# Mixture-of-experts stage: weight pieces released by the count of matrix products instead of in queue order with tiny transfers between

## The chip, the cores and the metric

One core of one Trainium2 chip runs the whole kernel. The metric is the device time of one execution in microseconds (us), as the median of several runs. One execution was also recorded by the hardware profiler; that is the profiled execution of the tables below.

## The reference, cut to what matters

The program is windowed attention followed by a mixture of experts. The change touches only the second half, the experts' two products:

```python
def _moe_ref(x, w_gate, w1, w2, capacity):            # x [3072, 512], 8 experts, F = 1024
    ...
    for e in range(E):
        ...                                           # at most capacity = 80 tokens an expert
        h = np.maximum(x[tok_idx] @ w1[e], 0.0)       # w1[e] [512, 1024]
        out[tok_idx] = gate_w[tok_idx, None] * (h @ w2[e])   # w2[e] [1024, 512]
```

The weights are float32: 8 experts x 2 matrices x 2 MB = 32 MB, read once from HBM.

## The kernel before, in words

The kernel has an attention stage (to about 190 us of the profiled execution), a short stage that ranks the tokens of each expert, and the expert stage, which the change is about.

**The experts' weights.** Each of the 16 matrices is loaded in two halves of 1 MB, each half in four pieces of 128 partitions x 512 float32 (256 KB): 32 halves, 128 pieces. The list `wsrc` (line 289) gives the order: w1 of expert 0, w1 of 1, w2 of 0, w1 of 2, w2 of 1 and so on. `load_weight` (line 298) takes the next half of that list, finds it a place, and issues its four transfers on SyncE's queue (line 320). There are 17 places for 32 halves (`NA, NB, NC = 6, 7, 4`, line 252): six in `wpool`, seven that come free in the attention's key and value buffers and beside them, four in `wpool3`, opened at the start of the expert stage (line 1295). Half n from 17 on takes the place of half n - 17, and its transfer waits until the products that read the old half are done. The first 13 halves are loaded during the attention and ranking stages; line 1196 issues one piece of a half and keeps the other three in the list `owed_parts`, which `load_owed` (line 330) issues later. 19 halves, 76 pieces, are left for the expert stage.

**The tiny transfers.** In the expert stage the list `spaced` is set (line 1306). Then `load_weight` issues, after some of the pieces, a transfer of a single float32 from `wg_t` in HBM to a small tile `spaced` (lines 321 to 325): three after every five pieces, so that of eight transfers in the queue five are weight pieces. Nothing reads that tile.

**The start of the expert stage.** GpSimd gathers the 80 token rows of an expert with an indirect DMA (`gather`, line 1309) into one of three buffers. Between the gathers of experts 1 and 2 and after them, `load_weight(hold=True)` puts a one-element memset on GpSimd's queue (line 313) that writes the place of the new half; the half's transfers must follow it, so they start after the gathers have been issued. Four halves are issued this way in the stage's head (lines 1315 to 1320); then SyncE loads a register with the flag for the fallback path (line 1321), and the rest of the halves are issued as `need` (line 1334) calls for them in program order.

**The products.** `ffn1(e)` (line 1361) computes h = relu(x w1) of one expert: 2 halves x 4 row blocks x 4 contraction blocks x 2 column halves = 64 calls of `pe.matmul` (line 1374). `ffn2(e)` (line 1381) computes the second product, again 64 calls (line 1392). The inputs are float32, and in the profile each call shows as two weight loads into the array (PEld) and two matmuls (PE). "Product" below means one call. There are 16 such stages of 64 products, in the order of `wsrc`: ffn1(0), ffn1(1), ffn2(0), ffn1(2), ffn2(1) and so on (lines 1434 to 1445). Stage j reads halves 2j and 2j + 1. Between them TensorE transposes gathered tokens (`tokens`, line 1347) and results (`rows`, line 1413). ScalarE applies the relu after each half of ffn1 (line 1378), and GpSimd writes finished rows with an indirect DMA (line 1426).

**What sets the order.** In the expert stage the order on every engine is the order of the program text (`manual_schedule`, lines 1303, 1307 and 1432); the scheduler adds the waits that the data need. SyncE's queue holds only the weight pieces and the tiny transfers there; gathers and writes are GpSimd's.

Of the kernel before, what the change touches and what calls it, by code (L numbers as in the profile page):

```python
# [8 lines left out]
F32 = mybir.dt.float32  # L9
# [10 lines left out]
B, H, S, D = 4, 8, 768, 64  # L20
# [3 lines left out]
P = 128  # L24
# [219 lines left out]
def attention_moe(ctx: ExitStack, tc, q, k, v, n_sink, window, w_gate, w1, w2, capacity, q_t, k_t, v_t, vs_t, wg_t, out):  # L244
    nc = tc.nc
# [50 lines left out]
    spaced = []  # L296

    def load_weight(hold=False, now=4):
# [13 lines left out]
        if hold:  # L312
            po.memset(t[0:1, 0:1], 0.0)
        to = t.rearrange("p (c f) -> p c f", c=src.shape[1])
        for n, i in enumerate(range(0, 2 * F, DM)):
            c, f = divmod(i, src.shape[2])
            if n >= now:
                owed_parts.append((to[:, c, f:f + DM], src[:, c, f:f + DM]))
                continue
            nc.sync.dma_start(to[:, c, f:f + DM], src[:, c, f:f + DM])  # L320
            if spaced:
                j = spaced[0]
                if 3 * (j + 1) // 5 > 3 * j // 5:
                    nc.sync.dma_start(spaced[1][0:1, j:j + 1], wg_t[0:1, 0, 0:1])
                spaced[0] += 1
# [968 lines left out]
    with ExitStack() as fctx:  # L1294
# [11 lines left out]
        spaced += [0, sm.tile([1, 4 * len(wsrc)], F32, name="spaced")]  # L1306
# [8 lines left out]
        for e in range(NG):  # L1315
            gather(e)
            if e > 0:
                load_weight(hold=True)
        while len(wtiles) < NA + NB + NC:
            load_weight()  # L1320
# [12 lines left out]

        def need(which, e):
            while (which, e, 1) not in wtiles:
                load_weight()
# [24 lines left out]
        def ffn1(e):  # L1361
# [3 lines left out]
            for half in range(2):  # L1365
# [5 lines left out]
                for f, c in todo:  # L1371
                    fc = half * (HC // 2) + f
                    for m in range(2):
                        pe.matmul(ph[m * D:(m + 1) * D, f], columns(0, e, c, fc * P + m * D), x[:, c],  # L1374
                                  start=(c == 0 and not (wide and f)), stop=(c == DC - 1), skip_group_check=True)
# [5 lines left out]
        def ffn2(e):  # L1381
# [6 lines left out]
            for dc in range(DC):  # L1388
                to = last if dc == DC - 1 else py
                for k in range(HC):  # L1390
                    for m in range(2):
                        pe.matmul(to[m * D:(m + 1) * D, dc], columns(1, e, k, dc * P + m * D), h[:, k],  # L1392
                                  start=(k == 0), stop=(k == HC - 1), skip_group_check=True)
                    if final and dc == DC - 1 and k == HC // 2:
                        rows_first(e)
# [38 lines left out]
        for e in range(E):  # L1434
            ffn1(e)
            if e % 2:
                for n in range(e + 1, min(e + 3, E)):
                    need(0, n)
# [65 lines left out]
```

## Time and profile before

| what | us |
|---|---|
| median of 3 runs | 292.58 (292.45 to 292.86) |
| the profiled execution's own time | 289.65 |
| span of its instructions | 287.9 |
| first product of the expert stage starts | 199.38 |
| last matmul starts | 281.88 |

All times of rows and of the text are counted from the start of the span of the profiled execution. PE is TensorE's matmul, PEld its load of weights into the array, DVE VectorE, ACT ScalarE, POOL GpSimd, SP SyncE; a q behind the name means the engine's queue of instructions (SPq). "L320" is line 320 of the kernel before. "x64" counts instructions. "<- issue" names idle time in which the engine waited for nothing that the profile shows. In the views of DMA, q1 holds the transfers of SyncE's queue, q0 the indirect ones of GpSimd, and q8 and q14 the engines' instructions; the last column is the time of their packets as a share of the 16 DMA engines' time.

### The profile page before, as it was taken

The numbers are of one execution on the slowest core, as the hardware profiler recorded it, in microseconds if no ns is written. First come the engines' busy times: TensorE is split into PE (matmuls) and PEld (weight loads), VectorE is DVE, ScalarE is ACT, GpSimd is POOL, SyncE is SP. The second block draws the span as 40 slices with busy tenths as digits, with TensorE's granted clock in tenths as the row PEclk, the third lists the DMA queues.
The fourth block names the chain that finished last, engine by engine and source line by source line (L and its number), as shares of the span: only waits on it lengthen the run. The fifth ranks groups of instructions, "written<-read, shape, count | busy, mean of one in ns | idle before, by whom it ended". The sixth has DMA issues, their size and how long they took to land.

```text
span 287.9 us, 11256 instructions
## 1 busy us (share of the span) xinstructions
PE 267.1 (93%) x4401; PEld 208.5 (72%) x4401; DVE 168.7 (59%) x566; ACT 165.9 (58%) x670; POOL 160.3 (56%) x365
## 2 busy tenths in 40 slices
PE   7889999999999999999899999998998999999991
PEld 2456777667776666776577767655988999999990
DVE  7678978778898988989996997880010010100001
ACT  3967988888988888785778787720111121221220
POOL 5876988668898679589758686636120030020211
PEclk9999999999999999999999999999999999999997
DMA  7999680999562999864275915597989899999811
GB/s 171 361 307 339 276 289 11 316 284 321 215 226 73 277 304 419 314 204 143 74 259 181 317 54 186 184 292 249 301 269 277 279 307 336 307 310 306 261 57 34
DMA packets 33366, 69.76 MB, mean 242 GB/s; under 512 B 4250, under 2 KB 6426, under 8 KB 32922
## 3 DMA queue, kind: packets, MB, share of 16 engines
q1 hardware_dynamic: 32282, 66.34, 69.4%
q0 software_dynamic: 1024, 2.62, 3.0%
q8 instruction: 37, 0.61, 0.9%
q14 instruction: 23, 0.19, 0.2%
HBM read 55.05 MB, written 13.89 MB: 239 GB/s over the span
## 4 chain that ended last, share of the span: by engine, by line
PE 36%; issue 21%; DVE 19%; ACT 14%; POOL 5%; DMA 3%; SPq 1%; ACTq 0%; POOLq 0%; DVEq 0%
ACT prob L607 9%; PE sc L570 7%; PE ph L1374 7%; PE pp L623 6%; PE xp L664 6%; DVE nm L597 3%; PE py L1392 3%; DVE sc L590 3%; ACT pt L635 3%; DVE gt L850 2%; POOL out_dram L1426 2%; DVE gt L847 2%; DMA kv_w<-in_moe_w_dram 1%; PE pr L697 1%; DVE sc L587 1%
## 5 line engine op out<-in xcount | busy, mean ns | idle before, releaser
L607 ACT ACTIVATE prob<-sc,nm 128x132 f32<-128x132 f32 (+1 forms) x192 | 68.9, 376 | 10.1 <-DVE nm L597 9.8
L570 PE MATMUL sc<-kv,q 64*64 64x196 f32 (+2 forms) x768 | 47.5, 335 | 8.0 <-ACT prob L607 6.0
L597 DVE TENSOR_REDUCE nm<-sc 128x2 f32<-128x264 f32 (+1 forms) x96 | 41.4, 431 | 3.3
L570 PEld LDWEIGHTS sc<-kv,q 64*64 64x64 f32 x768 | 21.3, 133 | 29.4 <-ACT prob L607 19.1
L635 ACT COPY pt<-pp 128x512 f32<-128x512 f32 x48 | 28.1, 585 | 24.1 <-PE pp L623 19.1
L590 DVE COPY_PREDICATED sc<-upper,sc 128x256 f32<-128x256 int8 x80 | 33.7, 422 | 13.0 <-PE sc L570 6.4
L607 ACT ACTIVATION_READ_ACCUMULATOR prob<-sc,nm 128x1 f32 x192 | 40.3, 210 | 0.0
L664 PE MATMUL xp<-pt,kv 128*64 128x128 f32 x384 | 37.0, 285 | 0.0
L643 POOL TENSOR_SCALAR_AFFINE_SELECT own<-pt 128x512 f32<-128x512 f32 (+1 forms) x48 | 27.6, 575 | 11.3 <-ACT pt L635 10.8
L1426 POOL DMA_INDIRECT out_dram<-y,idx x8 | 7.3, 918 | 44.8 <-ACT y L1420 40.4
L1357 DVE COPY xs<-px 128x320 f32<-128x320 f32 x7 | 3.2, 487 | 49.3 <-PE px L1352 49.3
L623 PE MATMUL pp<-ident,prob 128*128 128x128 f32 x192 | 31.4, 286 | 0.1
L664 PE MATMUL xp<-own,kv 128*64 128x128 f32 x320 | 31.1, 273 | 0.0
L650 POOL TENSOR_SCALAR_AFFINE_SELECT pt<-pt 128x512 f32<-128x512 f32 (+1 forms) x48 | 28.5, 593 | 3.3
L623 PEld LDWEIGHTS pp<-ident,prob 128*128 128x128 f32 x192 | 20.2, 141 | 13.6 <-issue 9.1
L1374 PE MATMUL ph<-xs,w 128*64 128x80 f32 x640 | 26.4, 233 | 0.6 <-issue 0.4
L1392 PE MATMUL py<-h,w 128*64 128x80 f32 x640 | 25.5, 233 | 0.8 <-issue 0.8
L714 POOL TENSOR_TENSOR xr<-xr,rs 128x512 f32<-128x512 f32 x21 | 22.4, 1067 | 5.9 <-ACT xr L702 5.8
L1378 ACT ACTIVATE h<-ph 128x320 f32<-128x320 f32 x16 | 7.0, 437 | 31.7 <-PE ph L1374 31.7
L1374 PEld LDWEIGHTS ph<-xs,w 128*64 128x64 f32 x640 | 24.1, 137 | 1.2 <-issue 0.8
L1392 PEld LDWEIGHTS py<-h,w 128*64 128x64 f32 x640 | 23.5, 137 | 1.7 <-issue 1.6
L1311 POOL DMA_INDIRECT xg<-x_rows,idx_in x8 | 7.9, 994 | 28.3 <-PE px L1352 26.2
(194 smaller groups left out, 532.2 us busy)
## 6 DMA issues: line engine op xcount, KB each, us to landing
w<-in_moe_w_dram SPq DMA_DIRECT2D x80, 256.0 KB, 4.7
kv_w<-in_moe_w_dram SPq DMA_DIRECT2D x48, 256.0 KB, 4.6
kv<-in_v_t_dram SPq DMA_DIRECT2D x12, 512.0 KB, 8.8
out_dram<-zeros SPq DMA_DIRECT2D x24, 256.0 KB, 5.4
x_rows<-xr SPq DMA_DIRECT2D x24, 256.0 KB, 2.1
q<-in_q_t_dram SPq DMA_DIRECT2D x11, 512.0 KB, 9.9
kv<-in_k_t_dram SPq DMA_DIRECT2D x3, 1584.0 KB
kv<-in_k_t_dram SPq DMA_DIRECT2D x2, 528.0 KB
```

The costliest lines, as they stand in the source:

```text
L570: pe.matmul(sc[m * D:(m + 1) * D, h, c0:c1], qs[g][r, hp, q0:q0 + D], ks[b][r, hp, k0 + c0:k0 + c1], start=True, stop=True, skip_group_che ...
L590: ve.copy_predicated(own, upper, sc[:, :, 0:P])
L597: ve.tensor_reduce(out=nm, in_=sc[:, :, lo_c:hi_c], axis=AX.X, op=ALU.max, negate=True)
L607: ac.activation(prob[:, a, h, p0:], sc[:, h, lo_c:hi_c], AF.Exp, bias=nm[:, h:h + 1], scale=1.0, accum_out=ssum[:, n, 2 * hp + h:2 * hp + ...
L623: pe.transpose(pp[:, a, h], prob[:, a, h, SINK:], ident)
L635: ac.copy(pt, st.pop((t, "pp")))
L643: po.affine_select(out=own[:, a0:], in_=pt[:, a0:], pattern=[[0, 2 - a0], [0, 2], [1, P]], compare_op=ALU.is_ge, fill=0.0, base=0, channel ...
L650: po.affine_select(out=pt[:, a0:], in_=pt[:, a0:], pattern=[[0, 2 - a0], [0, 2], [-1, P]], compare_op=ALU.is_gt, fill=0.0, base=0, channel ...
L664: pe.matmul(xp[h * D:(h + 1) * D, a * P:(a + 1) * P], val[:, (2 * hp + h) * D:(2 * hp + h + 1) * D], pr[:, a, h], start=False, stop=(a == ...
L714: po.tensor_tensor(xr, xr, gst[(i0, "rs")][:, n, :, None].to_broadcast([P, H, D]), ALU.mult)
L1374: pe.matmul(ph[m * D:(m + 1) * D, f], columns(0, e, c, fc * P + m * D), x[:, c], start=(c == 0 and not (wide and f)), stop=(c == DC - 1), ...
L1392: pe.matmul(to[m * D:(m + 1) * D, dc], columns(1, e, k, dc * P + m * D), h[:, k], start=(k == 0), stop=(k == HC - 1), skip_group_check=True)
```

## The change

The tiny transfers, the memsets that held the first halves back, and the issue of four halves at the head of the stage go. Every product of the expert stage now goes through `product`, which counts it. After each eleventh, `next_piece` hands out the next piece: it takes the first of `owed_parts` (opening the next half with `load_weight(now=0)` if that list is empty and the place of the half is free by the count of products), issues its transfer on SyncE's queue, and gives the scheduler a dependency of that transfer on the product. `need`, which is still called ahead of each stage, hands out pieces at once if the stage's halves haven't all been handed out. A call of `need` ahead of the tokens of later experts goes.

```diff
--- before.py
+++ after.py
@@ -293,9 +293,8 @@
     for n, held in ((NA, []), (NA + 4, [])):
         homes[n:n + 3] = [(held, m) for m in range(3)]
     in_home = []
-    spaced = []
-
-    def load_weight(hold=False, now=4):
+
+    def load_weight(now=4):
         n = len(wtiles)
         which, e, half = wsrc[n]
         src = (w1, w2)[which][e].rearrange("(g c p) f -> g p c f", g=2, p=P)[half]
@@ -309,8 +308,6 @@
             t = pool[0][:, m * 2 * F:(m + 1) * 2 * F]
         else:
             t = pool.tile([P, 2 * F], F32, tag=f"w{m}", name=f"w_{which}_{e}_{half}", bufs=1)
-        if hold:
-            po.memset(t[0:1, 0:1], 0.0)
         to = t.rearrange("p (c f) -> p c f", c=src.shape[1])
         for n, i in enumerate(range(0, 2 * F, DM)):
             c, f = divmod(i, src.shape[2])
@@ -318,11 +315,6 @@
                 owed_parts.append((to[:, c, f:f + DM], src[:, c, f:f + DM]))
                 continue
             nc.sync.dma_start(to[:, c, f:f + DM], src[:, c, f:f + DM])
-            if spaced:
-                j = spaced[0]
-                if 3 * (j + 1) // 5 > 3 * j // 5:
-                    nc.sync.dma_start(spaced[1][0:1, j:j + 1], wg_t[0:1, 0, 0:1])
-                spaced[0] += 1
         wtiles[(which, e, half)] = t
 
     owed_parts = []
@@ -1303,7 +1295,6 @@
         chain.enter_context(tc.manual_schedule(engines={ve.engine, po.engine}))
         for t in xgs:
             po.memset(t[0:1, 0:1], 0.0)
-        spaced += [0, sm.tile([1, 4 * len(wsrc)], F32, name="spaced")]
         chain.enter_context(tc.manual_schedule(engines={nc.sync.engine}))
 
         def gather(e):
@@ -1314,10 +1305,6 @@
 
         for e in range(NG):
             gather(e)
-            if e > 0:
-                load_weight(hold=True)
-        while len(wtiles) < NA + NB + NC:
-            load_weight()
         other_set = nc.values_load(other, min_val=0, max_val=1)
         gsel = sm.tile([CAP, E], F32, name="gsel")
         po.tensor_tensor(gsel, tab[:, 0], tab[:, 1], ALU.add)
@@ -1331,9 +1318,27 @@
         ps_xs = fctx.enter_context(tc.tile_pool(name="ps_xs", bufs=2, space=PSUM))
         HC, DC = F // P, DM // P
 
+        PACE, done = 11, []
+
+        def product(*args, **kw):
+            done.append(pe.matmul(*args, **kw).ins)
+            if len(done) % PACE == 0:
+                next_piece(done[-1])
+
+        def next_piece(behind):
+            if not owed_parts:
+                n, places = len(wtiles), NA + NB + NC
+                if n == len(wsrc) or n >= places and len(done) < 2 * HC * DC * ((n - places) // 2 + 1):
+                    return
+                load_weight(now=0)
+            to, src = owed_parts.pop(0)
+            tc.add_manual_dep(nc.sync.dma_start(to, src).ins, behind.name,
+                              mybir.DependencyInfo(mybir.DependencyClass.Sync, mybir.DependencyReason.DATA),
+                              reason="weights flow at the pace of the products")
+
         def need(which, e):
-            while (which, e, 1) not in wtiles:
-                load_weight()
+            while (which, e, 1) not in wtiles or owed_parts and list(wtiles)[-1][:2] == (which, e):
+                next_piece(done[-1])
 
         def columns(which, e, k, c0):
 
@@ -1371,7 +1376,7 @@
                 for f, c in todo:
                     fc = half * (HC // 2) + f
                     for m in range(2):
-                        pe.matmul(ph[m * D:(m + 1) * D, f], columns(0, e, c, fc * P + m * D), x[:, c],
+                        product(ph[m * D:(m + 1) * D, f], columns(0, e, c, fc * P + m * D), x[:, c],
                                   start=(c == 0 and not (wide and f)), stop=(c == DC - 1), skip_group_check=True)
                 if wide:
                     tokens(1)
@@ -1389,7 +1394,7 @@
                 to = last if dc == DC - 1 else py
                 for k in range(HC):
                     for m in range(2):
-                        pe.matmul(to[m * D:(m + 1) * D, dc], columns(1, e, k, dc * P + m * D), h[:, k],
+                        product(to[m * D:(m + 1) * D, dc], columns(1, e, k, dc * P + m * D), h[:, k],
                                   start=(k == 0), stop=(k == HC - 1), skip_group_check=True)
                     if final and dc == DC - 1 and k == HC // 2:
                         rows_first(e)
@@ -1435,7 +1440,6 @@
             ffn1(e)
             if e % 2:
                 for n in range(e + 1, min(e + 3, E)):
-                    need(0, n)
                     tokens(n)
                 for n in (e - 3, e - 2):
                     if n >= 0:
```

## Rows read from the trace of the kernel before

**Rows 1.** The page, busy time by engine: us (share of the span) and instructions.

```profile
PE 267.1 (93%) x4401; PEld 208.5 (72%) x4401; DVE 168.7 (59%) x566; ACT 165.9 (58%) x670; POOL 160.3 (56%) x365
```

**Rows 2.** Stretches: busy us (instructions) PE, PEld, DVE, ACT, POOL; clock; DMA share.

```profile
199.38:244.00 44.62, 42.65 (x1128) 41.09 (x1130) 2.27 (x5) 7.26 (x16) 6.95 (x9) 1.00 0.93 295
244.00:270.00 26.00, 26.00 (x715) 25.64 (x710) 0.89 (x2) 4.72 (x10) 1.82 (x2) 1.00 0.92 306
270.00:280.00 10.00, 10.00 (x252) 9.49 (x252) 0.00 (x0) 3.03 (x6) 2.74 (x3) 1.00 0.34 109
```

**Rows 3.** Waits of weight loads, 199.3:244 us: total, times, longest.

```profile
PEld ph L1374 <- issue: 1.7, 3, 0.9
PEld py L1392 <- issue: 1.3, 3, 0.7
```

**Rows 4.** Timeline of weight loads: start us, us, what, idle before.

```profile
205.91 3.38 PEld L1374 LDWEIGHTS ph<-xs,w 128*64 128x64 f32 x95 [0.30 <-issue]
209.38 0.61 PEld L1352 LDWEIGHTS px<-ident,xg 80*128 80x128 f32 x8
210.08 4.49 PEld L1392 LDWEIGHTS py<-h,w 128*64 128x64 f32 x128
214.49 0.91 PEld L1374 LDWEIGHTS ph<-xs,kv_w 128*64 128x64 f32 x24
216.27 3.66 PEld L1374 LDWEIGHTS ph<-xs,kv_w 128*64 128x64 f32 x104 [0.87 <-issue]
```

**Rows 5.** DMA queues, 213 to 215 us: packets, MB, share of the engines.

```profile
q8 instruction: 1, 0.02, 3.0%
```

**Rows 6.** Waits of the SyncE queue, 198:275 us: total, times, longest.

```profile
SPq L320 <- DMA w<-in_moe_w_dram: 16.4, 29, 1.8
```

**Rows 7.** Line 324, tiny transfers: ns min/median/max, first, last start.

```profile
L324 SPq DMA_DIRECT2D spaced<-in_wg_t_dram x45: 275/287/369, 199.0 to 268.9; - x45
```

**Rows 8.** Line 320: starts, then landing times, 200:226 and 243:270 us.

```profile
L320 SPq DMA_DIRECT2D w<-in_moe_w_dram x52: 327/328/1352, 198.0 to 269.7; - x52
...
DMA to landing us min/median/max: 3.7/4.5/6.7
...
DMA to landing us min/median/max: 4.1/4.4/5.0
```

**Rows 9.** Timeline of TensorE's matmuls: start us, us, what.

```profile
199.38 2.43 PE L1374 MATMUL ph<-xs,w 128*64 128x80 f32 x64
...
231.46 0.78 PE L1392 MATMUL py<-h,kv_w 128*64 128x80 f32 x16
...
256.44 0.45 PE L1374 MATMUL ph<-xs,w 128*64 128x80 f32 x8
...
260.87 4.60 PE L1392 MATMUL py<-h,kv_w 128*64 128x80 f32 x128
265.30 0.45 PE L1374 MATMUL ph<-xs,w 128*64 128x80 f32 x8
...
275.52 1.28 PE L1392 MATMUL py<-h,w 128*64 128x80 f32 x32
```

**Rows 10.** Waits of matmuls, 198:283 us: total, times, longest.

```profile
PE px L1352 <- DMA xg<-x_rows,idx_in: 1.0, 1, 1.0
```

**Rows 11.** DMA queues and pieces, 198:230 us, then 230:270 us.

```profile
q1 hardware_dynamic: 4282, 7.75, 76.9%
q0 software_dynamic: 400, 1.00, 11.1%
...
w<-in_moe_w_dram SPq DMA_DIRECT2D x33, 256.0 KB, 4.5
...
q1 hardware_dynamic: 6379, 11.51, 86.0%
q0 software_dynamic: 320, 0.82, 5.9%
```

**Rows 12.** The page, DMA issues: count, KB each, median us to landing.

```profile
x_rows<-xr SPq DMA_DIRECT2D x24, 256.0 KB, 2.1
```

## The prediction

> **What bounds the kernel now.** First the page's head, to know which engine to follow: TensorE is busy for 93% of the span [rows 1]. The diff touches only the expert stage, so next I read a table of stretches of that stage. From the first product at 199.38 us to 244 us TensorE is busy 42.65 of 44.62 us; from 244 to 270 us 26.00 of 26.00; from 270 to 280 us 10.00 of 10.00 [rows 2]. So this stage is bound by TensorE, and all that a better supply can give back there are the 44.62 - 42.65 = 1.97 us of holes before 244 us.
>
> What are the holes? The waits of TensorE's weight loads in that stretch put six, of up to 0.9 us, down to "issue", that is, to nothing that the profile shows [rows 3]. In the timeline of those loads two of them end at 205.91 and 216.27 us, each in the middle of a run on one product group, not where an expert or a weight half begins [rows 4]. Between the two lie 95 + 8 + 128 + 24 = 255 loads with as many matmuls: 510 instructions, twice 255. Such an even count speaks for the code itself, and the DMA view says how it comes: between 213 and 215 us one packet of the instruction queue is moved [rows 5], and the hole ends a little after, at 216.27 us. I read the holes as TensorE waiting for its next block of code, whose transfer shares the DMA engines with the weights. The stretch has 1128 matmuls [rows 2], so 1128 / 128 = about nine blocks.
>
> The weights keep those engines full. In the expert stage SyncE's queue waited 29 times, 16.4 us in all, for an older weight piece to land before it could issue the next [rows 6]. 45 tiny transfers stand among the 76 pieces, 0.287 us of the queue each [rows 7]: three in every eight transfers, so they hold places in the queue that weights would have. From issue to landing a piece takes 4.5 us (3.7 to 6.7) from 200 to 226 us and 4.4 us (4.1 to 5.0) from 243 to 270 us [rows 8]. 76 pieces between the first issue at 198.0 and the last at 269.7 us [rows 8] make 71.7 / 76 = 0.94 us each, so about 4.5 / 0.94 = 4.8 are under way at any time, call it five. The DMA engines are at a share of 0.93, and of 0.34 from 270 us on, where weights end and no hole is seen [rows 2].
>
> **The change, part by part.** (1) The 45 tiny transfers go: 45 x 0.287 = 12.9 us of SyncE's queue. That queue is not on the path, since it waits for landings 16.4 us; worth nothing by themselves. Their hidden effect is that up to eight pieces can be under way instead of five.
>
> (2) The hold memsets on GpSimd, and the early issue of pieces from 198.0 us, go. The first piece now waits for product 11. A product is two matmuls, so that is 22 matmuls after 199.38 us at 2.43 / 64 us each [rows 9]: 200.2 us, 2.2 us later. Nobody waits for it: 13 of 32 halves are loaded by then, enough for six stages of 64 products and half of a seventh, and the seventh starts at 231.46 us [rows 9]. TensorE's 1.0 us wait for the first gather [rows 10] is for a transfer issued ahead of all of this. I take 0; its ends are 0 and, if the pieces at 198.0 us hindered the gather's last part, a gain of all of that 1.0 us.
>
> (3) Each eleventh product signals SyncE, 76 times. The nearest rows: the stage that begins at 256.44 us signals ScalarE after each half, the one that begins at 260.87 us only at its end, and both take 4.43 us [rows 9]. So a signal costs 0, and at most the 0.01 us to which the rows are read, 0.8 us for 76. I take 0.
> The Trainium skill (TensorE: Matmul & The Clock Gate, "The cost: per-tile semaphore tail") states 26.3 ns per increment where every tile's matmul raises a semaphore; 76 of them would be 2.0 us, and the sum would turn from a gain into a loss. That was seen for tiles that run side by side, and the two equal stages above speak against it here.
>
> (4) SyncE's queue now waits for TensorE. Behind a waiting transfer stand only later pieces: gathers and writes are issued by GpSimd. The moved register load of the fallback flag also stands in an idle queue: 0. Would a piece come too late? 836 = 76 x 11 products stand before the last piece; 13 stages are 832 products and end at 265.30 us, so it goes out at about 265.6 us. Landing in 4.5 to 6.7 us, it is there at 272.3 us at the latest, and the last stage, which needs it, starts at 275.52 us [rows 9]. Cover: 3.2 us. For stage j (from 0) the last piece needed is number 8j - 44, out at product 88j - 484, against 64j when the stage starts: the lead 484 - 24j only falls, to 124 products at j = 15. Late weights cost 0 unless the pieces take over 9.9 us.
>
> (5) The depth of the queue. Asked for: by 231.46 us 384 products, 34 pieces in 31.3 us, 0.92 us each; over all, (265.6 - 200.2) / 75 = 0.87 us. Served: from 198 to 230 us the weight queue moved 7.75 MB at 76.9% beside 11.1% of GpSimd's queue [rows 11]; scaled from 88.0% to full this is 275 GB/s, 0.95 us for 262 kB. From 230 to 270 us 11.51 MB at 86.0 + 5.9% [rows 11] give 313 GB/s, 0.84 us. So early on demand outruns service by 0.03 us a piece, about one piece by 231 us, and later they are level. The pieces under way start from none. A 256 KB transfer on a lightly used queue lands in 2.1 us [rows 12], and the shortest weight piece took 3.7 us [rows 8]; over 0.92 us these are 2.3 and 4.0 pieces. So I expect 2 to 4 under way at first and 3 to 5 from 231 us, where before it is five throughout.
>
> (6) The holes. No row shows a fetch beside three or four pieces. The ends are: 1.97 us of holes left (they do not hang on the depth; gain 0), and none left (as from 244 us on; gain 1.97 us). Some five of about nine block starts before 244 us have a hole, and none of size from 244 us, where landing times stay within 5.0 us instead of reaching 6.7 us; so a modest shortening clears most. Against that, bursts beside gathers remain, and pieces now bunch with TensorE's fastest stretches. I take 0.8 us of holes left: gain 1.2 us.
>
> **Sum.** Only (6) counts: -1.2 us. The profiled execution took 289.65 us (span 287.9 us); 289.65 - 1.2 = 288.45 us. The median of the timed runs is 2.93 us above it at 292.58 us, and I carry the step over unchanged: **291.4 us**. What is late next is TensorE itself; the last write and the end follow it unchanged.
>
> **Rivals.** *No change, 292.6 us:* the fetch is slow for a reason that the weights' depth doesn't touch, and holes of about 2 us stay. For it: at the same five pieces under way there are stretches with holes and without. Against: they are gone where the DMA is quiet. The Trainium skill (DMA: Bandwidth & Descriptors, "Queues, rings and completion order") says that a DMA engine takes turns between queues packet by packet; by that a code fetch would not stand behind the whole depth of the weight queue, and this rival would be right. The trace shows late fetches but not what they stood behind.
>
> *Slower, 294.3 us:* the open depth. If pieces are served slower than the 0.92 us at which TensorE asks, from 200 to 231 us, up to eight come to be under way: at 0.95 us each 7.6 us of traffic, against 4.5 us. The fetch, in the same engines, comes later and TensorE stalls at most block starts. It limits itself, since a stalled TensorE asks for no pieces: the 33 pieces issued from 198 to 230 us [rows 11] came every 0.97 us, and to match that it stalls 34 x (0.97 - 0.92) = 1.7 us; the nine or so blocks after that, if they now have holes as the first nine had, add 2.0 us. So 3.7 us of holes instead of 1.97: +1.7 us. It decides when landing times pass about 6.5 us. Against it: demand and service are almost equal.
>
> *Signals cost TensorE:* (3) at the upper end of its rows gives 291.4 + 0.8 = 292.2 us. From 1.2 / 76 = 0.016 us a signal the gain is gone, and at 0.024 us the kernel is measurably slower, 291.4 + 1.8 = 293.2 us. Against it: the two equal stages of (3), and that these signals stand alone, eleven products apart.
>
> *The pace is not what it says:* if the dependency is coarser than a product, pieces come in bunches, and the sum is that of no change, 292.6 us.
>
> **Chances.** Forecast, with a gain of over 0.2% (0.6 us, about what a measurement of this kernel can tell from no change): 0.58. Slower by the open depth 0.15, by signals 0.04. No change: 0.18 by fetches that don't care, 0.05 by a pace that isn't one. So faster 0.58, same 0.23, slower 0.19. Range: down to 290.3 us (all holes gone, and 0.3 us of the gather's wait), up to 293.6 us, which takes in the no-change cases and the milder half of the slower one.
>
> **What the new profile would show.** Right: no tiny transfers; SyncE's queue waits for TensorE's products in place of landings; median landing time of a piece under 4.2 us; first piece near 200.2 us and last near 265 us; "issue" holes in front of TensorE's loads from 199 to 244 us of 0.8 us or less and still almost none later. Wrong: landing times over 6 us with larger holes (the slower rival); shorter landing times with the same holes (the fetch doesn't stand behind the weights); a stage of 64 products longer than 4.43 us without holes (signals); a wait for a weight piece at the start of a late stage (pace too slow).

## The result and the profile after

The changed kernel takes **294.12 us** (median of 10 runs, 292.84 to 295.45) against 292.36 us for the kernel before, run beside it (10 runs, 291.26 to 293.38): 1.0061 times the time before, with a 95% interval of 1.0039 to 1.0083. It is slower by about 1.8 us, and outside the predicted range of 290.3 to 293.6 us. The profiled execution took 293.49 us.

The head of the page of the changed kernel (busy us, share of the span, instructions):

```profile
span 291.8 us, 11257 instructions
...
PE 269.7 (92%) x4401; PEld 209.5 (72%) x4401; DVE 168.7 (58%) x566; ACT 165.8 (57%) x670; POOL 160.2 (55%) x363
```

TensorE still bounds the kernel [rows 1]. The table of stretches of the changed kernel, with the columns of [rows 2]:

```profile
199.35:244.00 44.65, 42.54 (x1119) 40.95 (x1121) 2.27 (x5) 7.26 (x16) 6.94 (x9) 1.00 0.91 302
244.00:270.00 26.00, 24.78 (x660) 23.88 (x658) 0.89 (x2) 4.28 (x9) 1.82 (x2) 1.00 0.92 305
270.00:280.00 10.00, 9.07 (x222) 8.41 (x219) 0.00 (x0) 2.43 (x5) 1.82 (x2) 1.00 0.24 79
```

Ahead of 244 us TensorE is idle 44.65 - 42.54 = 2.11 us, about as long as before (1.97 us). New are 1.22 us of holes from 244 to 270 us and 0.93 us from 270 to 280 us, where [rows 2] has none. What SyncE's queue waits for, from 198 to 274 us (total us, times, longest), and its weight pieces (issue cost in ns as minimum, median and maximum, first and last start, and landing times):

```profile
SPq L1335 <- PE ph L1324: 24.4, 31, 7.9
SPq L1335 <- PE py L1324: 15.2, 23, 2.4
...
SPq L1335 <- DMA w<-in_moe_w_dram: 0.9, 3, 0.5
```

```profile
L1335 SPq DMA_DIRECT2D w<-in_moe_w_dram x52: 327/328/1386, 200.4 to 268.3; - x52
...
DMA to landing us min/median/max: 3.8/4.9/6.7
```

The queue waits for products, and hardly for landings any more [rows 6]: the change does what it says. But a piece now takes 4.9 us to land (median), not less than the 4.4 and 4.5 us of [rows 8].

### Where the landing time comes from

The DMA view of one stretch, 213 to 229 us, of the changed kernel (packets, MB and share of 16 engines of each queue; then the issues, with the median landing time last):

```profile
q1 hardware_dynamic: 2874, 5.24, 94.3%
...
w<-in_moe_w_dram SPq DMA_DIRECT2D x21, 256.0 KB, 5.5
```

and the same view of the profile of before, same stretch:

```profile
q1 hardware_dynamic: 2284, 4.13, 82.9%
...
w<-in_moe_w_dram SPq DMA_DIRECT2D x16, 256.0 KB, 4.5
```

21 pieces in 16 us where there were 16. An uninterrupted stage takes 4.43 us for 64 products [rows 9], so eleven products ask for a piece every 4.43 x 11 / 64 = 0.76 us. The queue moves one in 16 x 0.262 / 5.24 = 0.80 us even with the engines full. So in this stretch pieces pile up: 5.5 us of landing time at 16 / 21 = 0.76 us each are seven under way, where before there were 4.5 / (16 / 16) = between four and five.

### Two kinds of stop

The timeline of the changed kernel's weight loads (start us, busy us, what, count, idle time ahead):

```profile
223.94 0.84 PEld L1324 LDWEIGHTS ph<-xs,kv_w 128*64 128x64 f32 x22
225.22 3.73 PEld L1324 LDWEIGHTS ph<-xs,kv_w 128*64 128x64 f32 x105 [0.45 <-issue]
...
230.63 0.61 PEld L1324 LDWEIGHTS py<-h,kv_w 128*64 128x64 f32 x16 [0.19 <-issue]
...
233.38 0.23 PEld L1324 LDWEIGHTS py<-h,w 128*64 128x64 f32 x4 [0.48 <-issue]
234.10 0.13 PEld L1324 LDWEIGHTS py<-h,w 128*64 128x64 f32 x1 [0.50 <-issue]
...
240.83 0.24 PEld L1324 LDWEIGHTS py<-h,w 128*64 128x64 f32 x4
241.81 4.34 PEld L1324 LDWEIGHTS py<-h,w 128*64 128x64 f32 x123 [0.74 <-issue]
```

The stops that end at 225.22 and 241.81 us (0.45 and 0.74 us) are of the kind that the prediction read as waits for code [rows 4]: they lie a multiple of about 128 loads apart. I call them **block stops**. Others of this kind end at 262.32 (0.42), 267.24 (0.44) and 272.22 us (0.50): 2.55 us in all. The two at 233.38 and 234.10 us are of a kind that the first profile of before doesn't have: two, sometimes three stops of about half a microsecond, 0.7 us apart, in stages 2, 6, 10 and 14 (counted from 0, as in the prediction; the expectations below count from 1 and call them the 3rd, 7th, 11th and 15th). I call them **pairs**. A stop of 0.19 us after the transposes of results is in every profile.

The pairs made the comparison of the two first profiles misleading, so before was profiled again (label `before_again`): it took 292.1 us and has the pairs too. Its table of stretches:

```profile
199.35:244.00 44.65, 43.04 (x1133) 41.38 (x1134) 2.51 (x6) 7.26 (x16) 7.00 (x9) 1.00 0.97 315
244.00:270.00 26.00, 25.24 (x684) 24.66 (x682) 0.89 (x2) 4.72 (x10) 1.82 (x2) 1.00 0.92 299
270.00:280.00 10.00, 9.34 (x219) 8.57 (x217) 0.00 (x0) 2.39 (x5) 1.83 (x2) 1.00 0.13 36
```

The waits of its weight loads from 199.9 to 290 us (total us, times, longest):

```profile
PEld py L1392 <- issue: 5.1, 14, 0.5
```

and of the changed kernel:

```profile
PEld py L1324 <- issue: 5.7, 15, 0.7
PEld ph L1324 <- issue: 1.4, 3, 0.5
```

All of the 5.1 us are pairs and the 0.19 us stops: this execution of before has no block stop over 0.15 us. The changed kernel has 7.1 us, 2.0 us more. Its first product starts at 199.35 us and that of `before_again` at 199.78 us, 0.43 us later; its last matmul starts at 285.86 us against 284.18 us, 1.68 us later. The waits account for that: 2.0 - 0.43 = 1.6 us. Between these two executions the loss is the 2.55 us of block stops, less the earlier start and somewhat shorter pairs.

### The profile page after: what moved, and what is told of

Read it like the earlier page. It is cut to its first block, busy times and chain, and to the rows that moved or that the text cites. A ratio compares the mean times of both kernels' runs of the same rounds, so it can differ in the third digit from the quotient of the medians.

```text
span 291.8 us, 11257 instructions
## 1 busy us (share of the span) xinstructions
PE 269.7 (92%) x4401; PEld 209.5 (72%) x4401; DVE 168.7 (58%) x566; ACT 165.8 (57%) x670; POOL 160.2 (55%) x363
## 4 chain that ended last, share of the span: by engine, by line
PE 37%; issue 22%; DVE 19%; ACT 13%; POOL 5%; DMA 3%; SPq 1%; ACTq 0%; POOLq 0%; DVEq 0%
ACT prob L599 9%; PE sc L562 7%; PE ph L1324 6%; PE pp L615 6%; PE xp L656 6%; DVE nm L589 3%; PE py L1324 3%; DVE sc L582 3%; ACT pt L627 3%; DVE gt L842 2%; POOL out_dram L1431 2%; DVE gt L839 2%; PE pr L689 2%; DMA kv_w<-in_moe_w_dram 1%; DVE sc L579 1%
## 5 line engine op out<-in xcount | busy, mean ns | idle before, releaser
L1324 PE MATMUL py<-h,w 128*64 128x80 f32 x640 | 27.3, 234 | 2.5 <-issue 2.5
L1324 PE MATMUL ph<-xs,w 128*64 128x80 f32 x640 | 27.5, 233 | 0.7 <-issue 0.6
L1324 PEld LDWEIGHTS py<-h,w 128*64 128x64 f32 x640 | 24.6, 137 | 4.3 <-issue 4.1
L1324 PEld LDWEIGHTS ph<-xs,w 128*64 128x64 f32 x640 | 25.4, 137 | 1.3 <-issue 0.9
L656 PEld LDWEIGHTS xp<-pt,kv 128*64 128x64 f32 x384 | 21.1, 136 | 3.5 <-POOL pt L642 0.2
```

The lines of the kernel that those rows point to most:

```text
L656: pe.matmul(xp[h * D:(h + 1) * D, a * P:(a + 1) * P], val[:, (2 * hp + h) * D:(2 * hp + h + 1) * D], pr[:, a, h], start=False, stop=(a == ...
L1324: done.append(pe.matmul(*args, **kw).ins)
```

## The experiments

Theory D (depth): block stops grow with the number of weight pieces under way. Rivals: S, the signals cost TensorE time; N, the block stops do not depend on the weights, and the loss is something else. The runs came in five batches, each on one chip with the kernel before beside it; ratios are to that (the quotient of the two medians can differ from them by somewhat over 0.001). The record numbers the chips 8, 15, 13, 5 and 5.

### Is it the depth?

**The changed kernel once more.** No edit.

> The changed kernel once more, with a new profile. In its first profile four stages of 64 products, the 3rd, 7th, 11th and 15th, took 5.45, 5.78, 5.63 and 5.56 us instead of 4.43 us, each by two stops of TensorE that stand in the middle of a block of code. If they belong to the kernel, all four are there again at the same place; if they were a chance of that execution, they are gone or elsewhere and the profiled execution is near 289.5 us. The median is 294.1 us, 0.6% above the kernel before, either way.

Measured: 293.93 us, ratio 1.0034 (1.0013 to 1.0056). Slower again, by less, and its profile has the pairs in all four stages again.

**Tiny transfers put back, pace kept.**

```diff
+        spaced = [0, sm.tile([1, 4 * len(wsrc)], F32, name="spaced")]
...
+            j = spaced[0]
+            if 3 * (j + 1) // 5 > 3 * j // 5:
+                nc.sync.dma_start(spaced[1][0:1, j:j + 1], wg_t[0:1, 0, 0:1])
+            spaced[0] += 1
```

> The changed kernel with the tiny transfers put back, three after every five pieces, so that at most five pieces are under way; pace and signals stay. Depth theory (code blocks come late behind up to eight pieces): back to the time before, about 292.4 us, landing times near 4.5 us. Signal theory (the products' signals stop TensorE): stays at about 294.1 us.

Measured: 292.50 us, ratio 1.0006 (0.9977 to 1.0034). The pace with the tiny transfers is not slower than before.

**The tiny transfers taken from the kernel before, nothing else.**

```diff
             nc.sync.dma_start(to[:, c, f:f + DM], src[:, c, f:f + DM])
-            if spaced:
-                j = spaced[0]
-                if 3 * (j + 1) // 5 > 3 * j // 5:
-                    nc.sync.dma_start(spaced[1][0:1, j:j + 1], wg_t[0:1, 0, 0:1])
-                spaced[0] += 1
```

> The kernel before without the tiny transfers, no pace: up to eight pieces are under way from 198 us on. Depth theory: landing times near 7 us, more and longer stops at the starts of code blocks, slower than the kernel before by 2 us or more (over 294.4 us). Signal theory: no change, 292.4 us.

Measured: 299.64 us, ratio 1.0244 (1.0206 to 1.0282). The timeline of its weight loads:

```profile
210.16 0.89 PEld L1386 LDWEIGHTS py<-h,w 128*64 128x64 f32 x24
213.17 3.66 PEld L1386 LDWEIGHTS py<-h,w 128*64 128x64 f32 x104 [2.12 <-issue]
216.75 0.90 PEld L1368 LDWEIGHTS ph<-xs,kv_w 128*64 128x64 f32 x24
220.74 3.66 PEld L1368 LDWEIGHTS ph<-xs,kv_w 128*64 128x64 f32 x104 [3.08 <-issue]
224.32 0.63 PEld L1386 LDWEIGHTS py<-h,kv_w 128*64 128x64 f32 x16
224.87 0.34 PEld L1386 LDWEIGHTS py<-h,w 128*64 128x64 f32 x7
226.48 0.40 PEld L1386 LDWEIGHTS py<-h,w 128*64 128x64 f32 x9 [1.26 <-issue]
```

and its DMA view from 213 to 229 us:

```profile
q1 hardware_dynamic: 2829, 5.15, 96.0%
...
w<-in_moe_w_dram SPq DMA_DIRECT2D x21, 256.0 KB
```

104 + 24 = 128 loads from one stop to the next, 104 + 16 + 7 = 127 to the third: a stop at every block from 213 to 260 us, of up to 3.08 us, nine of them with 10.9 us in all. As in the changed kernel, 21 pieces in 16 us. So the tiny transfers held this back, and the change took them away.

The kept trace also has every packet of the instruction queue (q8). They are of 16 KB, and one comes for each 128 loads and 128 matmuls. The start of the packet ahead of each block stop, beside the end of the stop (us):

| kernel | stop ends | packet starts |
|---|---|---|
| `before_open` | 213.17, 220.74, 226.48, 231.63, 238.18, 243.92, 249.04, 253.92, 259.88 | 210.57, 218.19, 224.04, 229.28, 235.89, 241.32, 246.66, 251.46, 257.33 |
| the change | 225.22, 241.81, 262.32, 267.24, 272.22 | 222.70, 239.53, 259.94, 264.19, 269.90 |

TensorE goes on 2.3 to 2.6 us after the packet has started, 3.1 us in one case of fourteen. So a block stop is a wait for code. The packet itself takes 0.9 to 1.2 us at the nine stops of `before_open` and 0.9 to 1.6 us in `before_again`, which has no block stop: the fetch is not slow, it starts late. Counted from the start of the block ahead, the packet starts after 2.4 to 5.0 us at those nine stops, after 0.8 to 2.7 us in `before_again`, and after 0.1 to 1.2 us in `before_open` from 260 us on, when its last weights land and no block stop is left.

**The same kernel, with five as the limit.** A piece now waits, by a dependency, until the fifth piece ahead of it has landed; no tiny transfer comes back.

```diff
-            nc.sync.dma_start(to[:, c, f:f + DM], src[:, c, f:f + DM])
+            piece = nc.sync.dma_start(to[:, c, f:f + DM], src[:, c, f:f + DM]).ins
+            if stage:
+                under_way.append(piece)
+                if len(under_way) > 5:
+                    tc.add_manual_dep(piece, under_way[-6].name,
+                                      mybir.DependencyInfo(mybir.DependencyClass.Sync, mybir.DependencyReason.DATA),
+                                      reason="pieces under way")
```

> The kernel before without tiny transfers (before_open, 2.4% slower), but each weight piece of the stage also waits for the landing of the fifth piece ahead of it. Depth theory: the number under way is what the tiny transfers set, so this is level with the kernel before (ratio 0.997 to 1.003). If the tiny transfers do something else (a pause in the queue, other places in it), it stays over 1.01.

Measured: 292.64 us, ratio 1.0015 (0.9988 to 1.0042). The same blocks in its timeline of weight loads:

```profile
211.71 1.09 PEld L1393 LDWEIGHTS py<-h,w 128*64 128x64 f32 x29 [0.47 <-issue]
213.18 2.63 PEld L1393 LDWEIGHTS py<-h,w 128*64 128x64 f32 x74 [0.38 <-issue]
...
215.79 4.44 PEld L1375 LDWEIGHTS ph<-xs,kv_w 128*64 128x64 f32 x126
...
224.77 4.75 PEld L1375 LDWEIGHTS ph<-xs,kv_w 128*64 128x64 f32 x128
...
237.03 4.47 PEld L1375 LDWEIGHTS ph<-xs,w 128*64 128x64 f32 x126
```

and the DMA view from 213 to 229 us:

```profile
q1 hardware_dynamic: 2417, 4.40, 86.3%
...
w<-in_moe_w_dram SPq DMA_DIRECT2D x17, 256.0 KB
```

Most blocks now pass without a stop: runs of 126 and 128 loads. What ends at 213.18 us belongs to a pair; the block stop of 2.12 us is still there at 211.71 us, with 0.47 us, and with two others (0.20 and 0.39 us) 1.1 us of block stops are left of 10.9. The weight bytes that are issued and not yet moved, read from the packets, make 3.0 pieces on average from 213 to 229 us, against 4.6 in `before_open`, 4.1 in the changed kernel, and 2.9 and 2.8 in the two profiles of before. (That is less than the pieces under way, which count until they have landed.) `before_open` lost 299.64 - 292.74 = 6.9 us to before on its chip, this kernel 292.64 - 292.13 = 0.5 us on its own, within its interval, and between the two nothing but the limit was changed. That is the test that decides for theory D against N at the size of `before_open`'s loss.

**The changed kernel, with five and with six as the limit,** and once more without one.

```diff
+            under_way.append(nc.sync.dma_start(to, src).ins)
+            if len(under_way) > 5:
+                tc.add_manual_dep(under_way[-1], under_way[-6].name,
+                                  mybir.DependencyInfo(mybir.DependencyClass.Sync, mybir.DependencyReason.DATA),
+                                  reason="pieces under way")
```

> The changed kernel, pace of eleven, where each piece also waits for the landing of the fifth piece ahead of it. Depth theory: level with the kernel before (0.997 to 1.003), as with the tiny transfers. If the pace itself costs, it stays at 1.003 to 1.008.

> The same with the sixth piece ahead. Depth theory: between five and the open pace, 1.001 to 1.006; that says how steep the cost is between five and eight.

> The changed kernel on the same chip as the three above, as their measure: 1.003 to 1.008 against the kernel before by the earlier runs. If this chip shows the pairs of stops beside back-to-back indirect transfers (as two chips did and two did not), its time is near 294 us, else near 291.5 us.

Measured, on one chip: five 291.99 us, ratio 0.9990 (0.9963 to 1.0017); six 292.80 us, 1.0008 (0.9981 to 1.0035); none 294.16 us, 1.0044 (1.0020 to 1.0068). The waits of SyncE's queue with five:

```profile
SPq L1335 <- DMA w<-in_moe_w_dram: 21.4, 33, 2.5
SPq L1335 <- PE ph L1324: 15.3, 17, 7.7
```

The limit does bind: the queue waits for landings again. The loss is gone, and no gain comes in its place; the limit is all that parts the 291.99 from the 294.16 us. Six came out level too, and the runs do not tell it from five. The table puts side by side the profiles that show pairs; "waits" is the sum of what the view of the weight loads' waits from 199.9 to 290 us gives to issue and to weights, "block stops" the part of it at the starts of blocks (stops from 0.2 us).

| kernel | profiled, us | waits, us | block stops, us | ratio to before |
|---|---|---|---|---|
| `before_again` | 292.10 | 5.1 | 0 | (before) |
| `pace_limit5` | 291.75 | 5.5 | 0.3 | 0.9990 |
| `open_limit5` | 292.71 | 5.5 | 1.1 | 1.0015 |
| `pace_limit6` | 292.22 | 5.8 | 0.9 | 1.0008 |
| `before_signals` (below) | 293.00 | 6.4 | 1.3 | 1.0007 |
| `pace_and_tiny` | 292.89 | 6.5 | 1.3 | 1.0006 |
| the change | 293.49, 293.92, 294.46 | 7.1, 7.2, 7.7 | 2.6, 3.5, 3.0 | 1.0061, 1.0034, 1.0044 |
| `ahead_13` (below) | 294.12 | 8.1 | 3.7 | 1.0091 |
| `before_open` | 301.13 | 13.7 | 10.9 | 1.0244 |

The profiled time less the waits is 286.0 to 287.4 us in every row, so what the kernels differ by, up to 9 us, lies in these waits to within 1.4 us. One profile by itself says little about a small loss, though: the first of before has five pieces under way, 2.8 us of block stops and no pairs.

### Do the signals cost?

60 of the pieces of before got a dependency on a product that was long done, to get signals without waits. Fewer came of it: in the traces 45 products of the expert stage raise a signal in before, 88 in this kernel and 105 in the change, so it tests 43 of the 60 that the change adds.

```diff
+                if 0 <= 11 * j - 100 < len(done):
+                    tc.add_manual_dep(piece.ins, done[11 * j - 100].name,
+                                      mybir.DependencyInfo(mybir.DependencyClass.Sync, mybir.DependencyReason.DATA),
+                                      reason="a product long done")
```

> The kernel before, with tiny transfers and without pace, but 60 of its 76 pieces also wait for a product that is long done (eleven products apart), so that TensorE raises 60 more signals and nothing is held back. Signal theory: slower by some 1.4 us (60/76 of 1.76 us), about 293.8 us, with stops that aren't at the starts of code blocks. Depth theory: no change, 292.4 us.

Measured: 292.74 us, ratio 1.0007 (0.9984 to 1.0029); 292.74 us was also the median of before. In the timeline of its matmuls one stage runs from 257.71 to 262.14 us:

```profile
257.71 0.49 PE L1339 MATMUL ph<-xs,w 128*64 128x80 f32 x8
...
262.14 4.17 PE L1339 MATMUL py<-h,kv_w 128*64 128x80 f32 x114
```

4.43 us, as in [rows 9]. 43/60 of the loss of 1.76 us would be 1.3 us, and the interval ends at 0.9 us. `pace_limit5`, which raises all of the change's signals, is level as well. Rival S is out.

### Shallower, and with a head start

**A tiny transfer after every piece,** so at most four pieces among eight transfers: the edit of `pace_and_tiny` with `if True:` for its condition.

> The changed kernel with a tiny transfer after every piece, so that at most four pieces are under way. Depth theory: stops at the starts of code blocks no more than with five, 291.5 to 292.7 us, unless the pieces then come late (a wait of TensorE for weights, over 293 us). If depth beyond five alone were the point, the same as with five: 292.5 us.

Measured: 300.32 us, ratio 1.0263 (1.0222 to 1.0304). The waits of its weight loads from 198 to 295 us:

```profile
PEld py L1325 <- issue: 5.8, 13, 1.4
PEld py L1325 <- DMA w<-in_moe_w_dram: 2.5, 5, 0.7
PEld py L1325 <- DMA kv_w<-in_moe_w_dram: 2.4, 4, 1.0
```

Four are too few here: the weights come late in the last three stages and TensorE waits for them. Up to 271 us there is no block stop, and the packets of code start 0.2 to 1.8 us into the block ahead. After the waits, from 286 to 291 us, the granted clock is 0.50 (the level of 1.2 GHz), and 84 weight loads that take 2.98 us in `before_again` take 5.30 us: some 2.3 of the 8.3 us are that. What serves is a narrow middle.

**Two halves issued ahead of the products (before issues four), and one piece per 13 products.**

```diff
+            if e > 0:
+                load_weight(hold=True)
...
-        PACE, done = 11, []
+        PACE, done = 13, []
```

> The changed kernel with two halves issued ahead as in the kernel before, and then one piece per thirteen products instead of eleven, without tiny transfers. At 13 products TensorE asks for a piece in about 0.90 us in its fastest stretches instead of 0.76 us, so the queue should not grow past four. Depth theory: back to the time before or better, 291.5 to 292.7 us. If it is the loss of the tiny transfers itself that costs, and not the depth, it stays at 294 us.

Measured: 294.77 us, ratio 1.0091 (1.0056 to 1.0126). Its timeline of weight loads:

```profile
212.90 3.66 PEld L1328 LDWEIGHTS py<-h,w 128*64 128x64 f32 x104 [1.84 <-issue]
...
218.82 3.66 PEld L1328 LDWEIGHTS ph<-xs,kv_w 128*64 128x64 f32 x104 [1.44 <-issue]
...
226.83 4.50 PEld L1328 LDWEIGHTS ph<-xs,kv_w 128*64 128x64 f32 x128
```

The stops stand at the start, where the eight pieces of the head start and the paced ones pile up: the bytes issued and not yet moved make 4.7 pieces on average from 206 to 213 us, 3.5 from 213 to 219 us, and 2.1 to 2.4 from 219 to 258 us. From 222 to 268 us, at the slower pace, no run of 128 loads is broken but by the pairs and the stops of 0.19 us. A miss against what was expected, but it shows the two sides in one execution.

### The pairs, and executions without them

**Before, profiled once more.** No edit.

> The kernel before once more, for a second profile; its first one took 289.65 us, below all of its timed runs. All profiles taken since (of the changed kernel and of three variants) show pairs of stops of TensorE in the 3rd, 7th, 11th and 15th stage, about a microsecond each time, beside two indirect transfers that GpSimd issues back to back; the first profile of the kernel before shows none. If the pairs are a matter of the execution, they are here too, and the profiled execution is near 292.5 us. If they came with the products' signals or the pace, they are not here.

Measured: 292.1 us; shown above. Here too the pairs lie beside two indirect transfers of GpSimd that start 1.27 us apart. In the changed kernel (timeline of POOL):

```profile
231.32 0.95 POOL L1431 DMA_INDIRECT out_dram<-y,idx  x1 [0.55 <-issue]
232.58 0.93 POOL L1431 DMA_INDIRECT out_dram<-y,idx  x1 [0.30 <-issue]
```

The stops that follow are those shown above, which end at 233.38 and 234.10 us.

**Before, with gathers and writes one at a time.**

```diff
+                if half == 0 and e > 1:
+                    rows(e - 2)
...
-            if e % 2:
-                for n in range(e + 1, min(e + 3, E)):
-                    need(0, n)
-                    tokens(n)
-                for n in (e - 3, e - 2):
-                    if n >= 0:
-                        rows(n)
+            if 0 < e < E - 1:
+                need(0, e + 1)
+                tokens(e + 1)
```

> The kernel before with the gathers and the writes of results moved apart: one expert's tokens and one expert's rows in each step, half a stage between them, instead of two and two in every second step. Theory that back-to-back indirect transfers stop TensorE in pairs: the four pairs go, some 3 to 4 us less, about 289 us. If the pairs have another cause, 292.5 us as before.

Measured: 289.66 us, ratio 0.9910 (0.9876 to 0.9944), the only kernel that beat before. Its timeline of POOL:

```profile
218.06 0.95 POOL L1428 DMA_INDIRECT out_dram<-y,idx  x1 [7.22 <-ACT y L1422]
220.06 0.97 POOL L1311 DMA_INDIRECT xg<-x_rows,idx_in  x1 [1.05 <-PE px L1352]
228.17 0.94 POOL L1428 DMA_INDIRECT out_dram<-y,idx  x1 [7.13 <-ACT y L1422]
```

The transfers are at least 2.0 us apart, and none of the pairs is left. Its waits in the view of the table sum to 2.1 us. But the edit also moves work of TensorE, and one of the six executions took 293.54 us, so this run alone does not show that the distance of the transfers did it.

**The same edit on the changed kernel, and half the head start with one piece per 12 products, without and with it.** `ahead_4_pace_12` is the edit of `ahead_13` with `e == 1` and 12.

> The changed kernel (pace of eleven products, no tiny transfers) with gathers and writes moved apart as in before_spread, so that the pairs of stops beside GpSimd's back-to-back transfers are gone. Depth theory: the stops at the starts of code blocks remain, 1.2 to 1.8 us above before_spread's 289.7 us, so 290.9 to 291.5 us, still faster than the kernel before. If the change cost time only through the pairs, it comes out at 289.7 us.

> The changed kernel with one half (four pieces) issued ahead and then one piece per twelve products, no tiny transfers. Depth theory: no burst of eight at the head and a slower ask, so the queue stays at four or a little more; fewer stops at the starts of code blocks than at eleven, 292.0 to 293.0 us, near the kernel before. If the pace itself or the missing tiny transfers cost, it stays near 294 us. If pieces come late at the end, TensorE waits for weights in the last stage.

> The same, with gathers and writes moved apart. If the two causes are separate they add: 2.4 to 3 us below ahead_4_pace_12, 289.2 to 290.3 us; level with before_spread.

Measured: 291.42, 291.13 and 291.05 us; ratios 1.0066 (1.0033 to 1.0098), 1.0064 (1.0034 to 1.0093) and 1.0059 (1.0032 to 1.0086). In this batch before took 289.41 us, and `ahead_4_pace_12`, which has the old order of gathers and writes, shows no pair at all, with writes 1.2 to 1.3 us apart. So there was nothing here for the spreading to remove, and the third expectation fails. The first is met in microseconds only, since before itself was 3 us faster than it assumed: the kernel is not faster than before. The second fails too: the profile of `ahead_4_pace_12` (292.37 us, the longest of its 12 executions) has 5.7 us of block stops, not fewer than at eleven.

**GpSimd kept busy between the two transfers,** by three memsets of an otherwise unused tile after each gather and write, to part them without moving work on TensorE.

> The kernel before with three memsets of a scratch tile on GpSimd after every gather and write of the two-and-two steps, so that indirect transfers are issued over 2.2 us apart, and nothing else moved. Theory of back-to-back indirect transfers: the pairs of stops go, about 289.5 us. If it was the moved work of TensorE or ScalarE in before_spread that did it, the pairs stay, 292.1 us.

Measured: 289.33 us, ratio 1.0004 (0.9967 to 1.0041). It ran in the same batch, where there were no pairs to part, so it tells nothing of them.

**Both ideas together:** the changed kernel with five as the limit and the transfers apart, and `before_spread` again.

> The changed kernel with the pace of eleven, at most five pieces under way by a dependency, and gathers and writes moved apart. Depth theory with separate causes: on a chip that shows the pairs of stops, level with before_spread, 0.988 to 0.995 of the kernel before; on one that doesn't, 0.997 to 1.003.

> The kernel before with gathers and writes moved apart, a second time: 0.988 to 0.995 of the kernel before on a chip that shows the pairs of stops, 0.997 to 1.003 on one that doesn't (the kernel before is then near 289.5 us).

Measured: 291.80 us, ratio 1.0070 (1.0030 to 1.0110), and 290.27 us, 1.0028 (0.9996 to 1.0060), beside 289.30 us for before. The second is as expected for this level of before, the first is a miss. So `before_spread` is 0.9% better where before takes 292 us and not better where it takes 289 us, and the paced kernel with a limit, level with before in the one case, loses 0.7% in the other. Why the paced kernels lose there, even with five as the limit, is open. The profile of `limit5_spread` does not settle it: it is of one of its longest executions (293.51 us) and has 3.3 us of block stops and, in the last stage, 0.7 us of waits that the view puts down to SyncE's queue.

Nor is it the chip that decides. This batch and the one before it bear the same chip number in the record, and before took 292.13 us in one and 289.30 us in the other. The very first profile of before, without pairs, took 289.65 us beside timed runs of 292.45 to 292.86 us. What sets the level, and the pairs with it, is open.

## Why the prediction was wrong

The forecast was a gain of 1.2 us from smaller holes; the kernel lost 1.76 us (294.12 - 292.36). Point by point:

- **(1) the tiny transfers** were called worth nothing in themselves, with the open depth as their hidden effect. Right, and `before_open` shows how much they held back: 2.4%.
- **(2) the later start** was costed at 0, with the first piece at 200.2 us: 200.4 us, and nobody waited. The first product starts at 199.35, 199.75 and 199.41 us in the three profiles of the change and at 199.38 and 199.78 us in the two of before: right, no difference beyond the scatter.
- **(3) the signals** cost nothing: right (`before_signals`, `pace_limit5`). The 76 signals it counts are 60 new ones in the trace, since 45 products raised one already and some of these serve both. The Trainium skill's 26.3 ns per increment (TensorE: Matmul & The Clock Gate, "The cost: per-tile semaphore tail") doesn't carry over to signals that stand alone between products.
- **(4) late weights:** none in the first two profiles of the change. In that of `again_2` the view puts one stop of 0.88 us down to a landing, but it ends at the start of a block, 2.2 us after a packet of code has started, as block stops do. The last piece went out at 268.3 us (predicted 265.6), later by the stops.
- **(5) the depth** is the step that failed. It said that demand is 0.92 us a piece early and 0.87 us over all, about level with the service (0.95 and 0.84 us), so that "2 to 4 under way at first and 3 to 5 from 231 us" are to be expected. The 0.92 us were a mean over 31 us, transposes and gathers' waits included. Between those, products ask every 0.76 us, faster than the 0.80 us of full engines, and seven pieces came to be under way from 213 to 229 us. A queue fills in the bursts, and a mean doesn't show it.
- **(6) the holes.** "I take 0.8 us of holes left" failed with (5): the block stops were 2.55 us in the first profile of the change, 3.5 and 3.0 us in the two others. The 1.97 us that were to be won were also those of one execution of 289.65 us, below every timed run. I carried a step from it to the median "over unchanged", though the 2.93 us between them was the sign that they differ in kind: `before_again`, which took 292.1 us as the timed runs do, has no block stop over 0.15 us, and instead the pairs, which the change doesn't touch. In that execution there was nothing to win, and the other kernels with five pieces under way had 0.3 to 1.3 us of block stops.

The reading of the holes as TensorE waiting for its next block of code was right: the table of packet starts shows it.

The rival "Slower, 294.3 us: the open depth", with a chance of 0.15, had the mechanism: demand above service, pieces piling up before 231 us, code coming late. That its time was within 0.2 us of the measured one is partly luck. It reckoned 3.7 us of holes, at most block starts, in place of 1.97; the first profile has five block stops of 2.55 us, one ahead of 231 us and four behind, in place of none in `before_again`. It was to decide from landing times of about 6.5 us, and a median of 5.5 us from 213 to 229 us sufficed. The rival "no change", for which the Trainium skill spoke (DMA: Bandwidth & Descriptors, "Queues, rings and completion order": turns packet by packet), fell with `before_open` and `open_limit5`: with the same queues and the same packets the stops come and go with the pieces under way. The traces say that a late fetch begins late and then takes its usual 1 us. When TensorE asks for it, and at what place it then waits, no view shows.

## What to carry to other kernels

A stream of prefetches that shares its DMA engines with something TensorE needs at once wants a limit on what is under way, not only a pace: in the batches in which before takes 292 us five pieces of 256 KB were right and six level with them, up to eight cost 2.4% without a pace and 0.3 to 0.6% with it, and up to four, with pace and tiny transfers, 2.6%. Where before takes 289 us the paced kernel with the limit still lost 0.7%. Set that limit by a dependency on an earlier landing (`open_limit5`), and compare demand and service within the fastest stretch, not over the stage. And where the profiled execution lies outside the timed runs, profile again before a hole of it is counted as winnable.

## What had not been expected of the hardware

- TensorE stops beside two indirect transfers that GpSimd starts within 1.3 us: two or three stops of about half a microsecond, four times in the expert stage, in some executions and not in others. With the transfers 2.0 us and more apart there were none (`before_spread`, 0.9910 in a batch that has them). The cause is open: the run that was to part the transfers without moving other work fell in a batch without the stops.
- Before took 292.0 to 292.7 us in some batches and 289.3 to 289.4 us in others; one batch of each kind bears the same chip number. With writes about 1.2 us apart, every profile near or above 292 us has the pairs but one (`ahead_4_pace_12`, from a batch of the second kind), and the first profile of before, 289.65 us, has none.
- A single block stop reached 3.08 us with the queue open, in a stretch in which the view names no wait for data.
- TensorE's code comes in packets of 16 KB, and TensorE goes on 2.3 to 2.6 us after the start of the one it waits for. A block of 128 loads takes 4.43 us without a stop, so by these numbers I estimate that a packet may start some 2 us into the block ahead before it costs time.
